# A new order and new engines for the first sixteen chunks of a gated recurrence with a feed-forward block

## The chip, the cores and the metric

The kernel runs on one core of one Trainium2 chip. The metric is the device time of one launch in microseconds (us). The core has five engines that work side by side, each through its own list of instructions, strictly in order: TensorE (PE, matrix products and transposes), VectorE (DVE), ScalarE (ACT, functions by table), GpSimd (POOL) and SyncE (SP, which here only issues DMAs). They wait for each other by semaphores alone.

## The reference

A linear recurrence over time runs through four sequences of 5824 tokens with 256 channels, and its output goes through a feed-forward block with a product in the middle and no nonlinearity:

```python
sig_r = 1.0 / (1.0 + np.exp(-r_gate)); sig_i = 1.0 / (1.0 + np.exp(-i_gate))
log_a = c * sig_r * np.log(np.clip(a_base, 1e-06, 1.0 - 1e-06))[None, None, :]
a_t = np.exp(log_a)
norm = np.sqrt(np.maximum(1.0 - a_t * a_t, 1e-06))
x_gated = norm * sig_i * x
for t in range(S):
    h = a_t[:, t] * h + x_gated[:, t]
    y[:, t] = h
a = y @ w1; b = y @ w2          # 256 -> 1024
return (a * b @ w3) @ w_out     # 1024 -> 1024 -> 256
```

All inputs and the output are float32. The kernel computes with bfloat16 operands on TensorE.

## The kernel before

The 23296 tokens are cut into 47 chunks, 0 to 46: chunks 0, 1 and 46 have 256 tokens, all others 512. Since nothing nonlinear stands between w3 and w_out, the kernel folds the two into one 1024x256 matrix `wp_sb` first (the eight "folds"), so each chunk needs only three products.

Nothing is left to a scheduler. A long string, `ORDER`, lists every job as a short word, and the kernel emits the jobs in exactly that order. Each engine so gets its own list: the words that belong to it, in the order of the string. Sets of tuples above the string (`DV_COPY`, `AC_SQUARE` and so on) say which engine does a job that several could do. The words, for chunk c, with the lines of the kernel before:

| word | job | engine (line) |
|---|---|---|
| r, i, x c | load of the r gate, the i gate, x, 512 KB each | SP (L136) |
| R, I c | tanh of the r gate (to bfloat16), of the i gate | ACT (L145/147, L154) |
| p c, t c.half | i gate plus 1; times x, to bfloat16 tile `u_t`; for chunks in `DV_TIMES` both in one | POOL (L159, L178) or DVE (L175, L178) |
| V, U c | turn tanh(r), turn u to channels x time | PE transposes to PSUM for chunks in `TURN_R` / `TURN_U` (L185), else a DMA transpose issued by SP (L196) |
| d c.half | decay a = exp(...) | ACT (L207) |
| s c.half | a squared | POOL or DVE (L217), ACT if in `AC_SQUARE` (L215) |
| q c | square root of 1 - a squared | ACT (L221), with its own function table |
| g c | times u | DVE (L229/232) |
| h c.half | the recurrence itself, a scan | DVE (L249) |
| y c | h to bfloat16 | POOL, DVE or ACT (L255/258) |
| a c.mp.q, b c.mp | quarter mp of y@w1 (one half each), of y@w2 | PE (L268) |
| c c.mp.q | copy of a from PSUM | DVE if in `DV_COPY` (L282), else ACT (L284) |
| m c.mp | product of the copy and b | DVE (L296) |
| D c.j, e c.j2, o c.j2 | product with `wp_sb`, copy from PSUM, store | PE (L307), ACT or DVE (L284/282), SP (L326) |
| L.., C.. | load and cast of weights | SP (L353); POOL, ACT or DVE (L360/362) |
| Ft, Fc, Fm, Fe mi | fold: 8 transposes, copy, 8 products, scale into `wp_sb` | PE (L367), DVE/ACT, PE (L378), DVE/ACT (L413/415) |
| W n | eight matmuls on nothing but the identity, whose result nobody reads | PE (L263) |

Tanh and exp share one of ACT's function tables and the root needs another, so ACT loads a table each time it goes from the one kind to the other. Copies and squares need no change of table.

Buffers are rings: `ring()` hands out the next slot of a tag each time a tile is taken, and a tile that comes back to a slot waits until the old content is done with. Four slots `po` of PSUM are shared by the turned gates, the folds, all `a` and all `D`; two slots `pb` by all `b` and `W`; three tiles `g` hold the products of three chunks, so m of chunk 3 cannot begin before D of chunk 0 is done. D needs all eight folds.

A chunk that is in both `TURN_R` and `TURN_U` is loaded with runs of 4 KB (`long_rows`), the others with runs of 1 KB.

## Time and profile before

| what | value |
|---|---|
| time, three runs | 515.61, 517.05, 517.40 us; median 517.05 us |
| profiled execution: its own time by the profile, the span from first to last instruction | 513.8 us |
| last matmul of TensorE | starts its last group at 507.24 us of the span |
| transposes for turned gates on PE (L185) | 104 |
| DMA transposes (L196) | 40 of r, 39 of u |
| DMA | 123.82 MB, mean 241 GB/s |

The three runs were not profiled, so the span is set beside their median: 3.2 us lie outside it. PE's matmuls overlap one another in the profile (each is shown with its whole time through the array), so what a matmul costs in a row of matmuls is the distance from one start to the next, not its duration. A few per cent of PE's matmul records are missing.

### The profile page before, as it was taken

To read this page: it belongs to the slowest core of one execution; us is meant where nothing else is said; L and a number is where in the kernel's file an instruction comes from. 1 tells how busy PE (TensorE), PEld (TensorE's weight loads), DVE (VectorE), ACT (ScalarE), POOL (GpSimd) and SP (SyncE) were. 2 spreads that over 40 slices of the span, in tenths; PEclk is the share of its full clock that TensorE was granted. 3 is DMA by queue.
4 is the path that set the end of the run, shared out by engine and by line. 5 is a ranking of instruction groups with operands and counts; after the bars stand their busy time and mean duration, and the time that the engine had idled before them with its cause. 6 is when DMAs were issued, how large, how long until landed. Compare 5 with 4: busy or idle time off the path is not lost.

```text
span 513.8 us, 9036 instructions
## 1 busy us (share of the span) xinstructions
PE 499.8 (97%) x3267; PEld 314.2 (61%) x3321; DVE 430.6 (84%) x414; ACT 465.5 (91%) x720; POOL 312.9 (61%) x271
## 2 busy tenths in 40 slices
...
GB/s 299 410 414 255 305 315 285 312 240 316 314 242 269 266 276 261 221 276 201 289 288 310 262 272 191 234 228 246 197 265 132 215 316 170 101 150 76 54 60 103
DMA packets 177281, 123.82 MB, mean 241 GB/s; under 512 B 86354, under 2 KB 172884, under 8 KB 177236
## 3 DMA queue, kind: packets, MB, share of 16 engines
...
## 4 chain that ended last, share of the span: by engine, by line
PE 86%; ACT 5%; DMA 4%; issue 2%; DVE 2%; SPq 1%; ACTq 0%; DVEq 0%
PE po L307 29%; PE pb L268 28%; PE pa L268 27%; DMA r_t<-in_r_gate_dram 4%; ACT sa L284 2%; PE pw L378 1%; PE ptr L185 1%; DVE g_t L296 1%; PE ptw L367 1%; ACT ot L284 1%; SPq L136 1%; DVE h_t L249 1%; ACT i_t L154 1%; ACT a_t L207 1%; ACT L154 0%
## 5 line engine op out<-in xcount | busy, mean ns | idle before, releaser
L296 DVE TENSOR_TENSOR g_t<-sa,pb 128x1024 bf16<-128x1024 bf16 (+1 forms) x188 | 219.0, 1181 | 62.0 <-PE pb L268 29.1
L268 PEld LDWEIGHTS <-w_sb 128*128 128x128 bf16 x1504 | 146.3, 98 | 146.8 <-issue 5.5
L284 ACT CAST sa<-pa 128x512 bf16<-128x512 f32 (+1 forms) x339 | 182.4, 588 | 27.6 <-PE pa L268 18.3
L268 PE MATMUL pa<-y_t,w_sb 128*128 128x512 bf16 (+1 forms) x721 | 185.9, 372 | 4.5 <-ACT sa L284 3.5
L268 PE MATMUL pb<-y_t,w_sb 128*128 128x512 bf16 (+1 forms) x729 | 182.5, 372 | 1.5
L307 PE MATMUL po<-wp_sb,g_t 128*128 128x256 bf16 x1456 | 177.7, 273 | 0.4
L307 PEld LDWEIGHTS <-g_t 128*128 128x128 bf16 x1456 | 142.4, 98 | 40.5 <-issue 0.9
L258 POOL CAST y_t<-h_t 128x1024 bf16<-128x1024 f32 (+1 forms) x46 | 51.2, 1112 | 141.2 <-DVE h_t L249 138.8
L178 POOL TENSOR_TENSOR u_t<-i_t,x_t 128x512 bf16<-128x512 f32 (+1 forms) x89 | 120.0, 1365 | 5.5 <-DMA ut<-u_t 2.5
L249 DVE TENSOR_TENSOR_SCAN h_t<-a_t,h_t,nrm 128x512 f32<-128x512 f32 (+1 forms) x92 | 121.0, 1345 | 1.9
L217 POOL TENSOR_TENSOR nrm<-a_t 128x512 f32<-128x512 f32 (+1 forms) x74 | 81.3, 1116 | 12.8 <-ACT a_t L207 9.9
L207 ACT ACTIVATE a_t<-rt,la 128x512 f32<-128x512 bf16 (+1 forms) x80 | 64.2, 821 | 0.0
L159 POOL TENSOR_SCALAR i_t<-i_t 128x1024 f32<-128x1024 f32 (+1 forms) x45 | 53.4, 1189 | 17.6 <-ACT i_t L154 17.6
L284 ACT COPY ot<-po 128x512 f32<-128x512 f32 (+1 forms) x85 | 49.6, 590 | 11.8 <-PE po L307 11.5
L232 DVE SCALAR_TENSOR_TENSOR nrm<-nrm,ut 128x1024 f32<-128x1024 f32 (+1 forms) x39 | 54.4, 1394 | 5.2 <-ACT nrm L221 5.2
L154 ACT ACTIVATE i_t<-i_t 128x1024 f32<-128x1024 f32 (+1 forms) x47 | 49.2, 1049 | 0.1
L221 ACT ACTIVATE nrm<-nrm 128x1024 f32<-128x1024 f32 (+1 forms) x47 | 48.4, 1040 | 0.2
L147 ACT ACTIVATE th_r<-r_t 128x1024 bf16<-128x1024 f32 (+1 forms) x40 | 42.6, 1065 | 0.0
L282 DVE CAST sa<-pa 128x512 bf16<-128x512 f32 (+1 forms) x37 | 21.9, 617 | 1.4 <-PE pa L268 1.1
L221 ACT ACT_TABLE_LOAD x17 | 21.8, 1283 | 0.4
L215 ACT ACTIVATE nrm<-a_t 128x512 f32<-128x512 f32 (+1 forms) x17 | 10.7, 648 | 0.1
L263 PE MATMUL warm<-ident 128*128 128x128 bf16 x128 | 10.2, 247 | 0.0
...
## 6 DMA issues: line engine op xcount, KB each, us to landing
...
```

Source lines behind the costliest of these rows:

```text
L154: nc.scalar.activation(out=t[:, :n, :], in_=t[:, :n, :], func=AF.Tanh, scale=0.5)
L159: (nc.vector if c in DV_PLUS else nc.gpsimd).tensor_scalar(t, t, 1.0, 1.0, op0=ALU.add, op1=ALU.mult)
L178: (nc.vector if (c, half) in DV_HALF else nc.gpsimd).tensor_mul(out=u, in0=t, in1=xt)
L207: nc.scalar.activation(out=a, in_=pr, func=AF.Exp, scale=la4[:, cb:cb + 1], bias=la4[:, cb:cb + 1])
L217: (nc.vector if (c, cb) in DV_SQUARE else nc.gpsimd).tensor_mul(out=n, in0=a, in1=a)
L221: nc.scalar.activation(out=T["n", c][:, :, :w], in_=T["n", c][:, :, :w], func=AF.Sqrt, scale=-1.0, bias=1.0)
L232: nc.vector.scalar_tensor_tensor(out=T["n", c][:, :, :w], in0=T["n", c][:, :, :w], scalar=1e-3, in1=T["pu", c][:, :, :w], op0=ALU.max, op1 ...
L249: nc.vector.tensor_tensor_scan(h[:, cb, :], a[:, cb, :], n[:, cb, :], init, ALU.mult, ALU.add)
L268: nc.tensor.matmul(out=dst[:, :w], lhsT=w_sb[:, cb, m * P:(m + 1) * P], rhs=T["y", c][:, cb, :w], start=(cb == 0), stop=(cb == NCB - 1))
L284: nc.scalar.copy(out=dst, in_=src_ps)
L296: nc.vector.tensor_mul(out=T["g", c][:, 2 * mp:2 * mp + 2, :w], in0=T["sa", c, mp][:, :, :w], in1=T["pb", c, mp][:, :, :w])
L307: nc.tensor.matmul(out=po, lhsT=T["g", c][:, k, j * P:(j + 1) * P], rhs=wp_sb[:, k, :], start=(k == 0), stop=(k == KD - 1), skip_group_che ...
```

## The change

It replaces the front of `ORDER`, up to its 701st word, by another arrangement of the same 701 words; the remaining 1763 words are the same. It moves jobs between engines by the sets. It takes chunks 7 and 12 out of `TURN_R` and chunk 5 out of `TURN_U`: V7, V12 and U5 become DMA transposes, and chunk 7 is loaded with runs of 1 KB. `W` stays at sixteen words of eight matmuls. Since halves of a job may now come in either order, a tile is taken by whichever half comes first ("if not in T") instead of by half 0; `pair` gives 2 for every chunk that uses it, and `FOLD_DMA` is empty, so neither changes an instruction.

The sets:

```diff
-    TURN_R = {0, 1, 2, 3, 4, 7, 12}
-    TURN_U = {0, 1, 2, 3, 4, 5, 6, 7}
+    TURN_R = {0, 1, 2, 3, 4}
+    TURN_U = {0, 1, 2, 3, 4, 6, 7}
     DV_TIMES = {0, 1}
-    DV_PLUS = set()
-    DV_HALF = {(2, 0)}
-    DV_SQUARE = {(0, 0), (1, 0), (10, 0)}
-    AC_SQUARE = {(1, 1), (2, 0), (2, 1), (3, 0), (4, 0), (4, 1), (6, 0), (8, 1), (9, 1), (11, 0), (11, 1), (12, 1),
-        (13, 0), (13, 1), (14, 0), (14, 1), (15, 1)}
-    DV_CAST = set()
-    AC_CAST = {4}
-    DV_COPY = {(0, 0, 0), (0, 1, 0), (0, 1, 1), (0, 3, 0), (1, 1, 0), (1, 1, 1), (1, 2, 0), (1, 2, 1), (1, 3, 0), (2,
-        0, 1), (2, 1, 0), (2, 1, 1), (2, 3, 0), (3, 0, 1), (3, 2, 0), (3, 2, 1), (4, 0, 0), (4, 1, 0), (4, 2, 0), (4, 2,
-        1), (5, 1, 1), (5, 2, 1), (6, 2, 0), (6, 2, 1), (6, 3, 1), (7, 0, 0), (7, 1, 1), (7, 3, 0), (7, 3, 1), (8, 1, 0),
-        (8, 2, 0), (9, 1, 0), (9, 1, 1), (9, 2, 1), (10, 0, 0), (10, 1, 0), (10, 1, 1)}
-    DV_EVAC = {(1, 0), (2, 0), (3, 1), (5, 1), (9, 0), (9, 1)}
-    FOLD_ACT = {('c', 7), ('e', 0), ('e', 1), ('e', 2), ('e', 3), ('e', 7)}
-    W_ACT = {('w2', 0), ('w3', 6)}
-    W_DVE = {('w1', 1)}
-    STAGE = {'w1': ['a', 'a'], 'w2': ['nrm', 'nrm'], 'wo': ['a', 'nrm'], 'w3': ['a', 'nrm', 'a', 'nrm', 'a', 'nrm',
-        'a', 'nrm']}
+    DV_PLUS = {2}
+    DV_HALF = set()
+    DV_SQUARE = {(1, 1)}
+    AC_SQUARE = {(2, 0), (2, 1), (3, 1), (4, 0), (4, 1), (5, 1), (6, 1), (7, 1), (8, 0), (8, 1), (10, 0), (10, 1),
+        (11, 0), (12, 0), (12, 1), (13, 0), (13, 1), (14, 0), (14, 1), (15, 1)}
+    DV_CAST = {0, 3}
+    AC_CAST = set()
+    DV_COPY = {(0, 0, 0), (0, 0, 1), (0, 1, 0), (0, 1, 1), (1, 0, 0), (1, 0, 1), (1, 1, 0), (1, 1, 1), (1, 2, 0), (1,
+        2, 1), (2, 0, 0), (2, 0, 1), (2, 1, 1), (2, 2, 1), (2, 3, 1), (3, 1, 0), (3, 1, 1), (3, 2, 0), (3, 2, 1), (3,
+        3, 0), (4, 0, 1), (4, 1, 0), (4, 1, 1), (4, 2, 1), (5, 0, 0), (5, 0, 1), (5, 1, 0), (5, 1, 1), (5, 2, 1), (6,
+        1, 0), (6, 2, 0), (6, 2, 1), (6, 3, 1), (7, 3, 0), (8, 0, 0), (8, 1, 1), (8, 2, 1), (8, 3, 1), (9, 0, 0), (9,
+        1, 0), (9, 1, 1), (9, 2, 1), (10, 0, 0), (10, 1, 0), (10, 1, 1)}
+    DV_EVAC = {(1, 0), (5, 1), (9, 0), (9, 1)}
+    FOLD_ACT = {('c', 3), ('c', 7), ('e', 2), ('e', 4), ('e', 5), ('e', 7)}
+    FOLD_DMA = set()
+    W_ACT = {('w2', 0), ('w2', 1), ('w3', 7)}
+    W_DVE = {('w1', 0), ('wo', 0)}
+    STAGE = {'w1': ['a', 'a'], 'w2': ['nrm', 'nrm'], 'w3': ['a', 'nrm', 'a', 'nrm', 'a', 'nrm', 'a', 'nrm'], 'wo':
+        ['a', 'nrm']}
```

The code, in one example of eight alike, and the two additions:

```diff
     def square(c, cb):
         w = sizes[c]
-        if cb == 0:
+        if ("n", c) not in T:
             T["n", c] = ring(held, [P, NCB, CT], F32, name="nrm", tag="nrm")
...
+    def pair(c, j2):
+        return min(2, sizes[c] // P - 2 * j2)
...
     def fold_t(mi):
+        if mi in FOLD_DMA:
+            T["w3t", mi] = ring(ffn, [P, KD, P], BF16, name="w3t", tag="w3t")
+            nc.sync.dma_start_transpose(out=T["w3t", mi], in_=T["w3b", mi][:, 0, :])
+            return
```

The start of the order:

```diff
-       r0 r1 E A3. A0. A1. i1 R1 R0 W3 V1 I1 V0 W13 W12 A2. W9 d1.0 d1.1 s1.0 i0 W15 I0 x0 t0.1 W14 d0.0 s0.0 s1.1
-       d0.1 s0.1 q0 x1 t1.1 Lw1.0 r3 Lw2.0 r2 q1 R3 Lw1.1 i2 W11 U0 g0 h0.0 Lw2.1 Cw1.0 W10 W2 U1 W0 W7 R2 W4 h0.1
-       Lw3.2 x2 g1 y0 W8 Lwo.0 Cw2.0 a0.1.0 a0.1.1 h1.0 c0.1.0 h1.1 a0.0.0 a0.0.1 V2 c0.1.1 d2.0 c0.0.0 W6 y1 b0.0
-       c0.0.1 d2.1 I2 Cw1.1 a1.0.1 a1.0.0 b0.1 a1.1.0 a0.2.0 c1.0.0 c1.0.1 Cw2.1 p2 a0.2.1 Cw3.2 m0.0 m0.1 c1.1.0
-       Lwo.1 b1.0 m1.0 t2.0 r4 W1 c0.2.0 a1.1.1 a0.3.0 t2.1 Cwo.0 W5 c1.1.1 Ft2 c0.2.1 a1.3.0 s2.0 b1.1 c0.3.0 b0.2
-       U2 a1.3.1 s2.1 Cwo.1 i3 Fc2 V3 x3 Lw3.0 q2 Lw3.1 i4 Lw3.4 m1.1 c1.3.0 Fm2 R4 g2 h2.0 h2.1 d3.0 Lw3.7 c1.3.1
-       m0.2 d3.1 Lw3.5 Fe2 a1.2.0 a0.3.1 b1.2 a1.2.1 I3 c0.3.1 V4 s3.0 d4.0 d4.1 b0.3 y2 c1.2.0 Cw3.0 c1.2.1 m1.2
-       a2.0.0 a2.1.0 b1.3 m0.3 a2.2.0 b2.0 m1.3 a2.2.1 c2.0.0 Lw3.3 a2.0.1 s4.0 c2.2.0 s3.1 p3 t3.0 c2.1.0 Cw3.1 Ft0
-       c2.0.1 c2.2.1 Fc0 m2.0 Cw3.4 b2.1 I4 s4.1 q4 r7 t3.1 a2.3.0 a2.1.1 Fm0 b2.2 p4 Cw3.5 c2.1.1 Ft4 c2.3.0 m2.1
-       Fe0 Ft1 a2.3.1 U3 Lw3.6 q3 Fc4 c2.3.1 Fc1 Fm4 Cw3.7 b2.3 Ft5 g3 Fe4 Fc5 Ft7 x4 Cw3.3 R7 r5 h3.0 h3.1 Fm1 Fm5
-       Fc7 Fe5 Ft3 Fm7 Fe1 Cw3.6 V7 Fe7 y3 Ft6 Fc3 d7.0 d7.1 Fc6 m2.2 Fm3 i6 r6 a3.1.0 Fe3 R5 Fm6 a3.1.1 c3.1.0
-       c3.1.1 t4.0 Fe6 t4.1 i7 i5 x5 U4 a3.0.0 R6 D0.0 a3.0.1 D0.1 I6 c3.0.0 e0.0 m2.3 g4 a3.3.0 a3.2.0 b3.0 h4.0
-       h4.1 b3.1 c3.0.1 m3.0 D1.0 a3.3.1 D1.1 I5 c3.3.0 y4 V5 r8 m3.1 a3.2.1 V6 b3.2 I7 e1.0 c3.2.0 c3.2.1 c3.3.1
-       b3.3 m3.2 m3.3 p5 a4.0.1 r9 a4.1.0 d5.0 d5.1 R8 d6.0 s6.0 s7.0 d6.1 p6 t5.0 p7 x6 x7 o0.0 a4.0.0 i10 V8 D2.0
...
+       r1 r0 i0 x0 i1 x1 Lw1.0 r2 A3. E A0. A1. A2. R1 R0 I0 t0.1 W2 W4 W9 V0 V1 W12 U0 W14 W3 W5 W13 W8 W10 d0.1
+       d1.0 d1.1 d0.0 I1 s1.1 t1.1 Cw1.0 s0.1 s0.0 s1.0 q0 q1 R2 i2 Lw2.0 I2 Cw2.0 U1 W11 W7 W15 g0 h0.1 h0.0 y0
+       a0.0.1 W6 g1 h1.1 h1.0 a0.0.0 a0.1.0 V2 W1 b0.0 y1 p2 c0.0.1 c0.0.0 a1.1.1 a1.1.0 c0.1.0 m0.0 b1.1 c1.1.1
+       c1.1.0 m1.1 d2.1 s2.1 d2.0 s2.0 q2 x2 Lw1.1 Lw3.2 t2.1 Cw1.1 t2.0 a1.0.1 a0.1.1 b0.1 a1.0.0 b1.0 c1.0.1 c0.1.1
+       m0.1 c1.0.0 m1.0 a0.2.0 a1.3.1 a0.2.1 a0.3.0 Lwo.0 Lw2.1 Lwo.1 r3 Cw3.2 Cwo.1 r4 c0.2.0 c0.2.1 c1.3.1 c0.3.0
+       Cwo.0 Cw2.1 U2 g2 W0 a1.3.0 Ft2 b1.3 a0.3.1 Fc2 Fm2 c1.3.0 R3 c0.3.1 m1.3 a1.2.0 V3 b0.2 b1.2 Fe2 R4 h2.0 h2.1
+       Lw3.0 Lw3.4 i3 x3 Lw3.1 Lw3.5 Lw3.7 Lw3.3 r7 Lw3.6 x4 i4 r5 m0.2 a1.2.1 V4 b0.3 c1.2.0 c1.2.1 m1.2 d3.0 d3.1
+       d4.0 d4.1 y2 s3.0 Cw3.0 Cw3.4 a2.0.0 a2.2.1 m0.3 c2.0.0 a2.0.1 b2.0 c2.2.1 a2.2.0 c2.0.1 m2.0 a2.1.0 Ft4
+       a2.3.0 Fc4 s4.0 I3 c2.2.0 c2.1.0 s4.1 a2.1.1 a2.3.1 c2.3.1 c2.1.1 c2.3.0 b2.2 Ft0 b2.1 s3.1 q3 q4 Fm4 p3 t3.1
+       t3.0 Cw3.1 m2.2 m2.1 Fc0 Ft1 Cw3.7 Fe4 Fc1 Cw3.5 U3 b2.3 Fm0 Ft5 Ft7 g3 Fe0 Fc5 Cw3.3 Fm1 h3.1 Fe1 h3.0 y3 Ft3
+       Cw3.6 Fm5 R7 Fc7 Fm7 Ft6 V7 r6 i6 Fc3 Fm3 Fe3 Fc6 m2.3 Fe7 Fe5 I4 a3.0.0 b3.0 a3.1.0 Fm6 c3.1.0 Fe6 R5 c3.0.0
+       d7.1 d7.0 a3.2.1 p4 t4.0 t4.1 c3.2.1 a3.2.0 a3.1.1 a3.0.1 U4 R6 c3.0.1 I6 i5 I5 V5 d5.0 r9 V6 c3.2.0 c3.1.1
+       s7.0 g4 h4.0 h4.1 D1.1 D0.1 D1.0 D0.0 b3.1 a3.3.1 a3.3.0 e1.0 d5.1 s7.1 e0.0 d6.0 R9 y4 r8 x5 p5 s6.0 s5.0
+       t5.1 t5.0 m3.0 a4.0.0 a4.1.0 b3.2 m3.1 c3.3.0 m3.2 s5.1 c4.0.0 c3.3.1 x7 x6 p6 t6.1 t6.0 r10 V9 b4.0 a4.0.1
+       a4.2.1 c4.1.0 c4.0.1 m4.0 b3.3 a4.1.1 m3.3 c4.1.1 a4.3.0 D2.1 b4.1 D2.0 c4.2.1 m4.1 b4.3 a4.3.1 a4.2.0 b4.2 R8
+       d6.1 s6.1 q7 q5 q6 e2.0 c4.3.0 c4.2.0 d9.1 U5 V8 o0.0 o1.0 i9 i8 i7 o2.0 d9.0 c4.3.1 D3.0 D2.2 D3.1 D2.3 U6 g5
...
```

## The prediction

> **What bounds the kernel now.** I read the page first: busy shares and the end of the work.
>
> ```profile
> span 513.8 us, 9036 instructions
> ...
> PE 499.8 (97%) x3267; PEld 314.2 (61%) x3321; DVE 430.6 (84%) x414; ACT 465.5 (91%) x720; POOL 312.9 (61%) x271
> ...
> PE 86%; ACT 5%; DMA 4%; issue 2%; DVE 2%; SPq 1%; ACTq 0%; DVEq 0%
> ```
>
> The third line is the chain that ended last: TensorE is 86% of it. But a busy PE is not a fast one, so I next took the timeline of PE over the first 30 us, and priced PE's list from it.
>
> ```profile
> 12.97 1.03 PE L268 MATMUL pa<-y_t,w_sb 128*128 128x256 bf16 x8
> ...
> 18.99 0.38 PE L268 MATMUL pa<-y_t,w_sb 128*128 128x256 bf16 x2 [1.10 <-ACT sa L284]
> ...
> 25.13 0.38 PE L268 MATMUL pa<-y_t,w_sb 128*128 128x256 bf16 x2
> 27.70 0.38 PE L268 MATMUL pa<-y_t,w_sb 128*128 128x256 bf16 x2 [2.19 <-ACT sa L284]
> 27.92 0.60 PE L268 MATMUL pb<-y_t,w_sb 128*128 128x256 bf16 x4
> 28.38 0.38 PE L268 MATMUL pa<-y_t,w_sb 128*128 128x256 bf16 x2
> 28.66 0.61 PE L185 MATMUL ptr<-ident,th_r 128*128 128x128 bf16 x8
> 29.10 0.60 PE L268 MATMUL pb<-y_t,w_sb 128*128 128x256 bf16 x4
> ```
>
> From start to start: eight transposes take 29.10 - 28.66 = 0.44 us (0.0557 each by the median of all), a matmul of 256 columns 0.109, one of 512 columns 0.2165. With these the whole list of PE (without W, which nobody reads) is 490.9 us. At 27.70 the list has done 8.9 us; the last matmul ends at 510.7. 510.7 - 27.7 = 483.0 us for the remaining 482.0: **after 27.7 us PE loses 1 us in all.** The 18.8 us lost lie before: 12.0 until the first useful product at 12.97, 6.8 between 12.97 and 27.70. At a2.0.0 (29.54, list at 10.6) the loss is 18.9, and at D0.0 (48.76, list at 29.9) still 18.9.
>
> Then the chain in order of time and ACT around the last wait:
>
> ```profile
> 13.91 10.40 DMA r_t<-in_r_gate_dram
> 24.37 1.28 ACT L145
> 25.67 1.06 ACT th_r L145
> ```
>
> The load of r4 lands at 24.3; R4 stands in ACT's list ahead of a copy that frees a PSUM slot, so PE waits 2.19 us. Last, the busy times by stage (us, then busy of PE, PEld, DVE, ACT, POOL, granted clock, DMA share, GB/s):
>
> ```profile
> 12.97:27.70 14.73, 10.30 (x113) 8.42 (x112) 12.36 (x21) 12.62 (x20) 7.50 (x8) 1.00 1.04 410
> 27.70:48.76 21.06, 20.90 (x196) 15.66 (x199) 18.19 (x27) 20.11 (x31) 15.76 (x15) 1.00 0.91 353
> 48.76:125.00 76.24, 75.78 (x491) 47.32 (x498) 74.43 (x79) 75.90 (x107) 50.26 (x45) 1.00 1.06 290
> ```
>
> From 48.76 to 125 PE, ACT and DVE are all full; PE can only come forward if ACT and DVE come forward too.
>
> **Part 1: three turns leave PE.** V7, V12 and U5 are 3 x 8 = 24 transposes: 24 x 0.0557 = **-1.34 us** on a list that has no gaps. *TensorE: Matmul & The Clock Gate*, Part 4, speaks of about 275 ns for such a transpose in a kernel; by that the sum here would be 24 x 0.275 = 6.6 us, an estimate from the page. The starts here stand 0.0557 apart, and the measurement decides. In their place SP issues three DMA transposes (1.28 us of issue each, landing 4.4 us later by the median). Of the gates of chunks 5 to 16 turned by DMA, the one with least room waits 2.2 us between landing and first reader and most wait 4 to 14, so I cost the three at nothing on the path; without that cover each costs up to the 4.4 us of its landing. The worst place is V7: in SP's list it waits for R7 with r6, i6, i5 and V5 behind it. By the walk below R7 ends near 40.8; r6 then lands near 44, R6 stands on ACT near 47, and before, the DMAs idle from 47.5 to 50 anyway. Decays from `rt` take 0.83 instead of 0.78 us: four of them, +0.2 us on ACT. Chunk 7's loads in 1 KB runs are not on the path: chunks 5 and 6 load so now.
>
> **Part 2: the first chunks.** I walk the new lists with the durations of before; landings by rank, since from 10.0 us on the DMAs land one 512 KB load each 1.25 us (w1.0 at 10.02, the tenth after it at 22.5).
> - Gates. R1, R0, I0, the four decays (0.45 each from 5.51), I1: ACT is at 7.9; table 1.28, q0 ends 9.85, q1 10.4 (before 10.78). w1.0 lands at 10.02 and is cast on DVE (0.6), g0 0.67, two scans 1.2, y0 on DVE (about 0.4, half of the 0.69 us cast of 1024): 12.95. The first product starts at **13.0, as before**.
> - ACT. Table, R2 (lands 11.3) 11.7 to 12.7, I2 to 13.6, cast of w2.0 (lands 13.8) to 14.8, two decays and two squares of chunk 2 (0.67, 0.56 each) to 17.3, table, q2 ends at **20.3; before 23.2**. R3 and R4 come later, when r3 (22.5) and r4 (23.8) are there: the two waits for loads (0.70 and 1.18) and the table load between are off the path.
> - DVE. g1, two scans to 14.8, p2 (0.6), six copies (0.31) and m0.0, m1.1 (0.6) to 18.2, m0.1, m1.0 to 20.3, cast of wo.0, g2 at 21.2 (before 23.8), two scans to 26.1 (27.4), y2 27.2 (28.5).
> - PE. b0.0 at 15.0, a1.1.1 waits for its slot until 15.8, U2 until 20.7 for the copy behind q2, b1.3 until 22.6 for the cast of w2.1, V3 until 25.3 for R3. a2.0.0 then starts at **27.8 with 11.1 us done: 16.7 lost, 2.2 less** than before. Going on alike (V4's slot, Fe4 and Fc7 on ACT cost PE 0.2 to 0.5 each), D1.1 starts at 48.7 with 31.6 done: 17.1 lost against 18.9. **-1.8 us.**
>
> All stretches here show a clock of 1.00 with PE gaps of up to 2.2 us; the walk's longest gap is the 1.8 us ahead of the first product, so the sum holds no loss of clock. *TensorE: Matmul & The Clock Gate*, Part 1, would speak against so thin a start: an idle window of about 3.4 us halves the clock until PE has been busy for about as long again; an estimate from the page is 3.4 us x 1/2 = 1.7 us more per fall. No run here shows one.
>
> **Part 3: do ACT and DVE follow?** Net of both lists in the changed part, by rows of before (start to start):
> - ACT: one weight cast and one fold copy more (0.95 each), four 512 squares (0.57) and two evacuations (0.53) more, against seven 512 copies (0.5), y4 (0.95), a 256 copy, a 256 square and an Fe (0.3 each), and the 0.2 above: nothing. Table loads stay as many. Its idle time until q12 falls from about 5.7 (1.3 is the start, 0.9, 0.7, 1.2 and 0.8 waits for loads and folds) to 2.5. ACT can be 3.2 us earlier.
> - DVE: seven 512 copies (0.6 each), a weight cast, y0, y3, a 256 copy and an Fe come, two evacuations, a fold copy, t2.0 (0.95) and two squares go; p2 is an operation that DVE did not do: its bounds are 0.69 (cast) and 1.26 (the 1024-wide g), and I take 0.6 start to start, as for the cast, the nearest. **+3.3 us.** Until m9.0 DVE idled 12.6 us; by the walk 6.2 stay. DVE can be 12.6 - 6.2 - 3.3 = 3.1 us earlier.
> - POOL gives up some 6 us and waits 18 us for h alone between 45 and 125: no bound.
>
> ```profile
> POOL y_t L258 <- DVE h_t L249: 18.1, 5, 4.3
> POOL i_t L159 <- ACT i_t L154: 11.7, 4, 5.1
> ```
>
> **Sum.** -1.34 - 1.8 = -3.1 us, just what ACT and DVE allow. Those two have no room left over 76 us, so I take 0.5 us of new stalls in chunks 5 to 15 (ends: -1.0, when the 1 us that PE loses now goes too, and +3, the 3.1 us of DVE room gone). **-2.6 us** on a span of 513.8: 511.2. The median of the runs is 3.2 us above the span; 517.05 - 2.6 = **514.4**.
>
> **Rivals.**
> - *The start is won and lost again.* ACT never waits between 45 and 125 and its work does not shrink. If chunks 5 to 15 hold jobs in a worse order, PE waits at PSUM slots until it stands where it stood; the 1.34 us of transposes then turn into waiting. For it: 75.9 of 76.2 us busy. Against: ACT's room of 3.2 us. Time 517.05 - 0 to 0.8: about 516.8.
> - *DVE becomes the bound: slower.* It takes 3.3 us more in the stage where it has 1.8 us of 76 free. If the 6.4 us of idle time that the walk saves in the first 45 us do not go, m9.0 starts 3.3 us later than its 116.8, and PE, two pb slots ahead at most, is held as long: 517.05 + 3.3 = 520.3. It decides from the point where DVE saves less than 3.3 us of idle time. Against: its longest early waits (1.43 us for the root of q0, 1.28 for b1.0) end sooner in the walk.
> - *The change does not do what it says*: excluded for the transposes, the new list has 24 fewer.
>
> **Numbers.** Forecast 0.66, won and lost 0.20, DVE-bound 0.14. A difference of 0.3%, 1.55 us, is about what these runs (spread 0.35%) can tell from none. The forecast case lies beyond it (513 to 515.5), the second within, the third beyond on the other side: faster 0.66, same 0.20, slower 0.14. The low end is ACT's 3.2 us and the 1 us of present stalls: 512.8. The high end reaches halfway into DVE's case, 518.6, which leaves some 0.05 below and 0.14 above.
>
> **What would show it.** Right: q2 ends near 20, a2.0.0 starts by 28.2, D1.1 by 49, L185 has 80 transposes, PE loses under 2 us after D1.1, the last matmul ends near 508. Wrong: PE gaps of over 1 us in 50 to 125 released by `sa`, `g_t` or `rt`; m9.0 later than 115; SP standing at V7 beyond 42 us while R6 or I5 wait for loads; a clock below 1.00 in the first 30 us.

## The result, and the profile after

The changed kernel takes **518.40 us** (median of 7 runs, 517.34 to 520.61); the kernel before, beside it on the same chip, 515.68 us (7 runs, 515.37 to 517.40). The ratio is **1.0046, with a 95% interval of 1.0026 to 1.0065**: slower by 0.46%, where 514.4 us and faster was forecast. In some executions of either kernel the clock stands at half for some 3.4 us of the start (the clock episode, see the last section); among those without it the median is 517.35 us for after (3 of the 7) and 515.5 to 515.8 us for before (in its four larger sets of executions), so the sign is the same and the difference some 1.7 us.

The page of after, lines as in the prediction:

```profile
span 516.5 us, 9044 instructions
...
PE 502.7 (97%) x3297; PEld 312.7 (61%) x3297; DVE 434.2 (84%) x420; ACT 466.6 (90%) x717; POOL 312.5 (61%) x267
...
PE 76%; ACT 7%; DMA 6%; DVE 5%; issue 2%; SPq 2%; POOL 1%; DVEq 0%; ACTq 0%; POOLq 0%
```

PE is again 97% busy, which says nothing. The chain that ended last says more: PE's share fell from 86% to 76%, and ACT, DMA and DVE took 7% of the span more. The span is 2.7 us longer although PE's list is 1.34 us shorter.

The timeline of PE over the first 31 us of after:

```profile
13.19 0.39 PE L271 MATMUL pa<-y_t,w_sb 128*128 128x256 bf16 x2 [1.14 <-DVE y_t L261]
...
20.70 0.38 PE L271 MATMUL pa<-y_t,w_sb 128*128 128x256 bf16 x2 [0.54 <-DVE sa L285]
...
25.54 0.62 PE L187 MATMUL ptr<-ident,th_r 128*128 128x128 bf16 x8 [0.38 <-ACT th_r L147]
...
27.98 1.46 PE L271 MATMUL pa<-y_t,w_sb 128*128 128x512 bf16 x6
```

The 2.19 us gap before R4 is gone, and chunk 2's first product starts at 27.98 instead of 29.54. The stretch tables of after, in the windows used for before (busy of PE, PEld, DVE, ACT, POOL, granted clock, DMA share, GB/s):

```profile
12.97:27.70 14.73, 12.34 (x134) 10.18 (x135) 14.35 (x27) 14.39 (x22) 7.28 (x7) 1.00 1.04 409
27.70:48.76 21.06, 21.06 (x182) 14.29 (x180) 20.17 (x31) 20.45 (x28) 14.85 (x15) 1.00 0.88 315
48.76:125.00 76.24, 73.82 (x474) 45.27 (x471) 72.93 (x77) 72.20 (x102) 43.05 (x40) 1.00 1.09 286
```

In the first row PE is busy 12.34 us instead of 10.30: the start was won. In the third, PE falls from 75.78 to 73.82, and ACT from 75.90 to 72.20: engines that were full now wait. For what, the waits from 45 to 130 us tell (us in total, times, longest):

```profile
POOL u_t L180 <- DMA x_t<-in_x_dram: 4.4, 2, 3.3
ACT a_t L209 <- DMA rt<-th_r: 2.3, 3, 0.9
DVE nrm L234 <- DMA ut<-u_t: 2.1, 2, 1.7
PE pb L271 <- DVE g_t L299: 1.9, 1, 1.9
PE pa L271 <- ACT sa L287: 1.8, 3, 1.1
ACT th_r L149 <- DMA r_t<-in_r_gate_dram: 0.9, 1, 0.9
```

In before, ACT and DVE wait for no DMA at all in this stretch, and POOL 0.3 us once. Here ACT waits 3.5 us (0.3 us of it for an i gate) and DVE 2.1 us for transfers, and PE then waits for copies and products that stand behind them. One by one, the waits are 0.38 us for V6, 0.32 for i8, 0.37 for U5, 0.95 for V12, 1.74 for U9, 0.93 for V15 and 0.90 for r17. Only U5 and V12 are turns that the change moved: 1.3 of 5.6 us. The other 4.3 us are waits for transfers that the kernel before makes as well, and does not wait for. Set against PE's list, PE now loses 6.7 us between the end of the start and chunk 46; before it lost 0.9 us there. (Summed again, the lists are 490.6 and 489.3 us; the prediction's 490.9 is 0.3 too high, which changes none of its differences.)

| us | before | predicted | after |
|---|---|---|---|
| q2 ends | 23.2 | 20.3 | 20.39 |
| a2.0.0 starts; PE has lost by then | 29.54; 19.0 | 27.8; 16.7 | 27.98; 17.0 |
| lost at the end of the start (D0.0 / D1.1, 48.7) | 19.0 | 17.1 | 17.2 |
| PE's list | 490.6 | -1.34 | 489.3 |
| lost between there and chunk 46 | 0.9 | about 1.5 | **6.7** |
| ACT's work until q12 | 129.7 | 0 more | 130.55 |
| DVE's work until m9.0 | 104.2 | 3.3 more | 107.16 |

### The profile page after: what moved, and what is told of

It reads as the page before. It is cut to its first block, busy times and chain, and to the rows that moved or that the text cites. A ratio compares the mean times of both kernels' runs of the same rounds, so it can differ in the third digit from the quotient of the medians.

```text
span 516.5 us, 9044 instructions
## 1 busy us (share of the span) xinstructions
PE 502.7 (97%) x3297; PEld 312.7 (61%) x3297; DVE 434.2 (84%) x420; ACT 466.6 (90%) x717; POOL 312.5 (61%) x267
## 4 chain that ended last, share of the span: by engine, by line
PE 76%; ACT 7%; DMA 6%; DVE 5%; issue 2%; SPq 2%; POOL 1%; DVEq 0%; ACTq 0%; POOLq 0%
PE pb L271 25%; PE pa L271 25%; PE po L313 24%; ACT sa L287 2%; DVE h_t L252 2%; DVE g_t L299 2%; DMA i_t<-in_i_gate_dram 2%; DMA r_t<-in_r_gate_dram 1%; DMA x_t<-in_x_dram 1%; PE pw L389 1%; ACT a_t L209 1%; SPq L198 1%; DMA out_dram<-ot 1%; SPq L138 1%; DVE sa L285 1%
## 5 line engine op out<-in xcount | busy, mean ns | idle before, releaser
L287 ACT CAST sa<-pa 128x512 bf16<-128x512 f32 (+1 forms) x331 | 178.2, 587 | 27.0 <-PE pa L271 18.5
L271 PE MATMUL pa<-y_t,w_sb 128*128 128x512 bf16 (+1 forms) x752 | 189.8, 372 | 4.8 <-ACT sa L287 2.0
L271 PE MATMUL pb<-y_t,w_sb 128*128 128x512 bf16 (+1 forms) x752 | 185.0, 372 | 2.6 <-DVE g_t L299 2.3
L180 POOL TENSOR_TENSOR u_t<-i_t,x_t 128x512 bf16<-128x512 f32 (+1 forms) x90 | 123.5, 1389 | 12.5 <-DMA ut<-u_t 4.6
L209 ACT ACTIVATE a_t<-rt,la 128x512 f32<-128x512 bf16 (+1 forms) x84 | 67.3, 817 | 2.7 <-DMA rt<-th_r 2.7
L234 DVE SCALAR_TENSOR_TENSOR nrm<-nrm,ut 128x1024 f32<-128x1024 f32 (+1 forms) x40 | 56.8, 1421 | 7.3 <-ACT nrm L223 4.8
L287 ACT COPY ot<-po 128x512 f32<-128x512 f32 (+1 forms) x87 | 50.7, 589 | 12.0 <-PE po L313 11.7
L156 ACT ACTIVATE i_t<-i_t 128x1024 f32<-128x1024 f32 (+1 forms) x47 | 48.7, 1042 | 1.3 <-DMA i_t<-in_i_gate_dram 1.2
L149 ACT ACTIVATE th_r<-r_t 128x1024 bf16<-128x1024 f32 (+1 forms) x42 | 44.5, 1059 | 1.0 <-DMA r_t<-in_r_gate_dram 0.9
L285 DVE CAST sa<-pa 128x512 bf16<-128x512 f32 (+1 forms) x45 | 26.4, 624 | 0.3
L217 ACT ACTIVATE nrm<-a_t 128x512 f32<-128x512 f32 x20 | 12.6, 636 | 0.2
```

Source lines behind the costliest of these rows:

```text
L180: (nc.vector if (c, half) in DV_HALF else nc.gpsimd).tensor_mul(out=u, in0=t, in1=xt)
L209: nc.scalar.activation(out=a, in_=pr, func=AF.Exp, scale=la4[:, cb:cb + 1], bias=la4[:, cb:cb + 1])
L234: nc.vector.scalar_tensor_tensor(out=T["n", c][:, :, :w], in0=T["n", c][:, :, :w], scalar=1e-3, in1=T["pu", c][:, :, :w], op0=ALU.max, op1 ...
L271: nc.tensor.matmul(out=dst[:, :w], lhsT=w_sb[:, cb, m * P:(m + 1) * P], rhs=T["y", c][:, cb, :w], start=(cb == 0), stop=(cb == NCB - 1))
L287: nc.scalar.copy(out=dst, in_=src_ps)
```

## The experiments

The question was where some 5.7 us between 50 and 150 us come from. The candidates, some with a letter in the expectations (C, D and G are explained there): **A**, the hole that SP's wait at V7 leaves in the transfers; **B**, the DMAs, full since before, which now get three turned tiles more, so that the new order's gates land too late; **E**, ACT's work is the bound; **F**, the order of DVE's and ACT's jobs by itself. "Lost later" is what PE loses between D1.1 and the first product of chunk 46, by the prices of the prediction, in the one profiled execution of each kernel.

| run | built on | ratio to before [95%] | lost later, us |
|---|---|---|---|
| before | | 1 | 0.9 |
| after | | 1.0046 [1.0026, 1.0065] | 6.7 |
| e1_loads_first | after | 1.0043 [1.0026, 1.0060] | 6.9 |
| e2_v7_on_pe | after | 1.0105 [1.0088, 1.0122] | 5.6, after 2.1 more in the start |
| e8_u5_pe | after | 1.0118 [1.0090, 1.0146] | 8.3 |
| e3_before_v7_dma | before | 1.0011 [0.9999, 1.0024] | 1.4 |
| e16_before_u5_dma | before | 1.0031 [1.0017, 1.0046] | 2.8 |
| e4_new_start_old_rest | both | 1.0071 [1.0057, 1.0086] | 5.6 |
| e5_g9_later | after | 1.0099 [1.0079, 1.0119] | 9.3 |
| e6_late_readers | after | 1.0089 [1.0063, 1.0114] | 8.5 |
| e9_no_act_squares | after | 1.0036 [1.0024, 1.0048] | 6.2 |
| e11_squares_pool | after | 1.0056 [1.0043, 1.0070] | 8.1 |
| e7_thin_stores | after | 1.0025 [1.0010, 1.0039] | 5.6 |
| e10_fewer_loads | after | 0.9974 [0.9962, 0.9987] | 4.3 |
| e14_fewer_loads_and_r | after | 0.9964 [0.9951, 0.9977] | 2.4 |
| e13_before_fewer_loads | before | 1.0008 [0.9993, 1.0022] | 0.5 |
| e15_fewer_loads_g9_later | after | 1.0091 [1.0071, 1.0111] | 8.6 |
| e12_before_copy_first | before | 0.9987 [0.9973, 1.0000] | 0.7 |

### The hole at V7

SP stands at V7 for 9.1 us, until 40.81, and the DMAs run dry behind it. The wait of SP's queue in after, and the stretch 41 to 44 us:

```profile
SPq L198 <- ACT w3t L287: 9.1, 1, 9.1
```

```profile
41.00:44.00 3.00, 3.00 (x33) 2.52 (x31) 2.39 (x4) 2.87 (x5) 0.00 (x0) 1.00 0.51 96
```

96 GB/s, where before moved 398. e1 puts the three loads ahead of V7:

```diff
-        Cw3.6 Fm5 R7 Fc7 Fm7 Ft6 V7 r6 i6 Fc3 Fm3 Fe3 Fc6 m2.3 Fe7 ... c3.0.1 I6 i5 I5 V5
+        Cw3.6 Fm5 R7 Fc7 Fm7 Ft6 r6 i6 i5 V7 Fc3 Fm3 Fe3 Fc6 m2.3 Fe7 ... c3.0.1 I6 I5 V5
```

> The changed kernel, with the words r6, i6, i5 moved ahead of V7: three loads are issued before SyncE stands waiting for R7. Nothing else moves. Theory A (the new wait of SP at V7, 9.1 us from 31.7 to 40.8, leaves the DMAs half empty from 38 to 44, and chunks 5 to 15 then get loads and turned gates just in time): the stretch 38 to 44 fills up, the loss of PE after D1.1 falls from 6.7 us to 3 or less, the span from 516.5 to about 513. Theory B (three more DMA transposes are too much for DMAs that are full from 45 to 130 anyway, wherever they stand): the loss stays above 5 us. Theory C (the new order of chunks 5 to 15 is worse for ACT and DVE by itself): unchanged, 516 to 517.

The same stretch of e1:

```profile
41.00:44.00 3.00, 3.00 (x33) 2.53 (x31) 2.42 (x4) 2.87 (x5) 0.00 (x0) 1.00 1.51 338
```

The hole is filled, yet at 60 us the DMAs have moved hardly more than in after (20.39 and 20.27 MB). The waits for V6 and U5 are gone, but the large stalls are the same: 1.9 us at b7.1 and 1.5 at a10.2.0. A falls as the cause by itself.

### One turn at a time

e2 and e8 give V7, or U5, back to PE in the new order; e3 and e16 take V7, or U5, to the DMAs in the old one. V12 alone was not tried.

```diff
-    TURN_R = {0, 1, 2, 3, 4}
+    TURN_R = {0, 1, 2, 3, 4, 7}
```

> The changed kernel with chunk 7 back in TURN_R: V7 is again 8 transposes on PE (0.45 us), SyncE does not wait for R7, chunk 7 loads runs of 4 KB again. Theory A: like the kernel with the three loads ahead of V7, span about 513. Theory B: one of three transposes and its DMA time gone, a third of the loss: span about 515. Theory C: 516.5 to 517.

```diff
-    TURN_U = {0, 1, 2, 3, 4, 6, 7}
+    TURN_U = {0, 1, 2, 3, 4, 5, 6, 7}
```

> The changed kernel with U5 back on PE (8 transposes, 0.45 us), a DMA transpose less. Theory B: a third of what the turns add goes, span 515 or less. Theory D: its wait at g5 (0.4 us) goes and the 0.45 us come back: no change, 516 to 517.

Both are slower still, by new stalls. PE's timeline of e2, then of e8:

```profile
48.21 1.03 PE L389 MATMUL pw<-wo_sb,w3t 128*128 128x256 bf16 x8 [0.95 <-ACT a_t L209]
```

```profile
68.11 1.14 PE L313 MATMUL po<-wp_sb,g_t 128*128 128x256 bf16 x9 [2.12 <-ACT sa L287]
```

A turn on PE holds one of the four `po` slots until ACT's decays (or DVE's g) have read it, and the new list has no slot free at these places: in e2 the fold Fm6 waits for the decays of chunk 7. So this pair says nothing on what the DMA turns cost. The old order does:

```diff
-    TURN_R = {0, 1, 2, 3, 4, 7, 12}
+    TURN_R = {0, 1, 2, 3, 4, 12}
```

> The kernel before with chunk 7 taken out of TURN_R and nothing else: V7 becomes a DMA transpose, and in the old list too it stands ahead of i6, r6, i7, i5, x5 and waits for R7 (ends at 41.6). Theory A: the same hole in the DMAs, here with five loads behind it, in an order that is not laid out for it: PE loses 2 to 6 us more, span 515.5 to 519.5. Theory B: one more transpose, up to 2 us slower. Theory C: 0.45 us faster, 513.4.

```diff
-    TURN_U = {0, 1, 2, 3, 4, 5, 6, 7}
+    TURN_U = {0, 1, 2, 3, 4, 6, 7}
```

> The kernel before with U5 alone turned by DMA (eight transposes fewer on TensorE, one DMA transpose more, chunk 5 not otherwise changed). The prediction's costing (a turn is worth -0.45 us and its DMA costs nothing): ratio 0.999, stalls after D1.1 as before, 0.9 us. Theory B: with the old order's room of 3 us and more at the gates it also costs little, 0.999 to 1.001. If a DMA turn costs by itself whatever the order (rival), chunk 5's g waits for it and the ratio is 1.002 or more.

V7 makes no difference that can be told from none. But at a cost of nothing it would have gained the 0.45 us by which PE's list is shorter, ratio 0.9991, and that lies outside its interval: its turn costs about what it saves, or more. U5 costs 0.31% although PE's list is 0.45 us shorter. DVE's timeline of e16, then PE's:

```profile
67.42 1.23 DVE L232 SCALAR_TENSOR_TENSOR nrm<-nrm,ut 128x1024 f32<-128x1024 f32 x1 [1.52 <-DMA ut<-u_t]
```

```profile
72.30 0.59 PE L268 MATMUL pa<-y_t,w_sb 128*128 128x512 bf16 x2 [1.35 <-POOL y_t L258]
```

U5 is issued 0.03 us after t5 and lands 3.5 us later. DVE is free for g5 1.5 us before that, and PE stands for y5 behind g5 and its scans. Here a DMA turn does stand on the path, by its own landing time.

### The new start before the old rest

e4 takes the first 274 words of the new order, then the old order with its engines, V7, V12 and U5 on PE. It changes too many words for a short diff; the sets of chunks 0 to 3 are the new ones, and:

```diff
-    TURN_R = {0, 1, 2, 3, 4}
-    TURN_U = {0, 1, 2, 3, 4, 6, 7}
+    TURN_R = {0, 1, 2, 3, 4, 7, 12}
+    TURN_U = {0, 1, 2, 3, 4, 5, 6, 7}
```

> The new order with its engines up to the word ahead of D1.1 (274 words), then the old order with its old engines for all words that are left; V7, V12 and U5 on PE as before. So the new start without a wait of SyncE for R7, and without the new order of chunks 5 to 15. Theory A and B: the 1.8 us won in the start stay, span about 512, up to 1 us lost at the seam. Theory C: the same. If the start is worth nothing because ACT and DVE cannot follow (the second case of the prediction): 513.8.

The lead lasts until 45 us; then PE waits 1.1 us at Fm6 and, by its timeline, here:

```profile
65.63 0.59 PE L266 MATMUL pa<-y_t,w_sb 128*128 128x512 bf16 x2 [2.43 <-ACT sa L282]
```

Here the earlier start is of no use to a rest that was arranged for the later one. By a6.0.0 PE has lost 22.8 us, against 18.9 in before. Neither ACT nor DVE waits for a transfer between 45 and 130 us in e4, so an order that does not fit loses 5.6 us without any late gate.

### Moving the job that waits, or those behind it

In after, DVE does g8, h8, g9 and h9 in a row ahead of m7.2, for which b7.1 waits. DVE's timeline of after, and PE's:

```profile
93.93 1.22 DVE L234 SCALAR_TENSOR_TENSOR nrm<-nrm,ut 128x1024 f32<-128x1024 f32 x1
95.25 2.46 DVE L252 TENSOR_TENSOR_SCAN h_t<-a_t,h_t,nrm 128x512 f32<-128x512 f32 x2
99.45 1.22 DVE L234 SCALAR_TENSOR_TENSOR nrm<-nrm,ut 128x1024 f32<-128x1024 f32 x1 [1.74 <-DMA ut<-u_t]
100.78 2.46 DVE L252 TENSOR_TENSOR_SCAN h_t<-a_t,h_t,nrm 128x512 f32<-128x512 f32 x2
103.15 2.33 DVE L299 TENSOR_TENSOR g_t<-sa,pb 128x1024 bf16<-128x1024 bf16 x2
```

```profile
104.40 1.02 PE L271 MATMUL pb<-y_t,w_sb 128*128 128x512 bf16 x4 [1.86 <-DVE g_t L299]
```

g9 waits 1.74 us for the turned tile of U9, and 5 us later PE waits 1.86 us. e5 moves g9 behind:

```diff
-        ... V14 g8 h8.0 h8.1 g9 h9.1 h9.0 y9 y8 t10.0 t10.1 t11.1 t11.0 p13 m7.2 b7.1 m7.3 e5.1 ...
+        ... V14 g8 h8.0 h8.1 y8 t10.0 t10.1 t11.1 t11.0 p13 m7.2 b7.1 m7.3 g9 h9.1 h9.0 y9 e5.1 ...
```

> The changed kernel with the words g9, h9.1, h9.0, y9 moved behind m7.3 and nothing else. Now DVE stands from 93.9 to 103.2 at g8, h8, g9, h9, waits 1.7 us in it for the turned u of chunk 9 (DMA), and PE waits 2.03 us at b7.1 for the products behind it. Theory D (what costs the time is the order on DVE and ACT: readers of DMA-turned gates placed ahead of work that PE waits for, while their data land just in time): the stall of 2 us at b7.1 goes, DVE's wait at g9 falls under 0.5, span about 514.5, unless the stalls at 126 to 128 (ACT waits for r17, V15) take over what was won: 515.5. Theory B (the DMAs are too full, whatever the order): the wait moves with g9, and under 0.7 us is won.

The wait only changes its place. PE's timeline of e5, then the stretch behind the stall:

```profile
110.86 0.59 PE L271 MATMUL pa<-y_t,w_sb 128*128 128x512 bf16 x2 [3.32 <-DVE ot L285]
```

```profile
110.86:114.30 3.44, 3.44 (x11) 1.34 (x11) 3.44 (x5) 2.93 (x3) 0.53 (x1) 0.66 1.01 325
```

e5.1, which frees a `po` slot, now stands behind g9 and h9. The granted clock (the number after the five engines) falls to 0.66 behind the stall: an episode at half clock of 3.41 us, which after does not have at this place, costs some 1.7 us of the 9.3 (half of 3.41, an estimate). So 9.3 is not the price of the stall alone; the same holds for e6 and e15 (clock 0.57 and 0.55 behind theirs). e6 also moves three readers of gates later on ACT:

```diff
-        ... V12 d12.1 R14 d13.0 D6.3 D6.2 a7.1.1 a7.1.0 e6.1 d13.1 c7.1.0 c7.1.1 b7.2 ...
+        ... V12 R14 d13.0 D6.3 D6.2 a7.1.1 a7.1.0 e6.1 d13.1 c7.1.0 c7.1.1 d12.1 b7.2 ...
-        ... d15.1 m8.3 a9.2.0 c9.1.0 b9.2 c9.1.1 R16 a9.2.1 ...
+        ... m8.3 a9.2.0 c9.1.0 b9.2 c9.1.1 R16 d15.1 a9.2.1 ...
-        ... D8.0 R17 t12.1 ... e8.0 c10.0.1 g11 ...
+        ... D8.0 t12.1 ... e8.0 c10.0.1 R17 g11 ...
```

> As the one with g9 later, and on ACT three readers of late data moved back as well: d12.1 behind c7.1.1, d15.1 behind R16, R17 behind c10.0.1. Theory D: the three waits of ACT at DMAs (0.9 us each at 100, 118 and 125 us) shrink and the two stalls of PE at 126 and 128 (1.8 us) go too: span about 512.5, below the kernel before by about 1 us. Theory B: waits come back at other readers; span above 515.

It does not help: 3.6 us at the same a8.1.1. So the expectation that the order of these readers could be mended by itself failed both times.

### ACT's work

e9 leaves out the fifteen squares on ACT in chunks 5 to 15 (8.4 us of work; the root then takes 1 - a, so the outputs are others):

```diff
+        if (c, cb) in AC_SQUARE and 5 <= c <= 15:
+            return
```

> The changed kernel without the 15 squares that ACT does in chunks 5 to 15 (the root is taken of 1 - a there; left out of the computation): 15 x 0.56 = 8.4 us less work on ACT between 50 and 145, nothing moved. Theory E (ACT is the bound of this stage: up to q12 it works 0.85 us more than before, and each wait for a DMA, 3.5 us after 48.7, is paid in full because it has no idle time to give; PE follows it, +3.0 us): PE's loss after D1.1 falls from 6.7 to 2 or 3 us, span about 512.5. Theory F (DVE is the bound, with its 3 us of new work): loss stays above 5 us, span over 515.

If ACT's work were the bound, all 5.7 us should go. The time moves by 0.1% of before's, no more than the intervals leave open. The waits of e9 from 45 to 130 us:

```profile
ACT a_t L209 <- DMA rt<-th_r: 3.2, 3, 1.2
ACT i_t L156 <- DMA i_t<-in_i_gate_dram: 2.1, 2, 1.2
DVE nrm L237 <- DMA ut<-u_t: 2.0, 2, 1.3
ACT th_r L149 <- DMA r_t<-in_r_gate_dram: 2.0, 1, 2.0
```

ACT's waits for DMAs rise from 3.5 us to 7.3: with less to do it arrives sooner at gates that have not landed. E falls, and the waits point to B. e11 gives squares of chunks 7, 8, 10 and 12 (five in all) to POOL instead, with nothing left out:

```diff
-    AC_SQUARE = {(2, 0), (2, 1), (3, 1), (4, 0), (4, 1), (5, 1), (6, 1), (7, 1), (8, 0), (8, 1), (10, 0), (10, 1),
-        (11, 0), (12, 0), (12, 1), (13, 0), (13, 1), (14, 0), (14, 1), (15, 1)}
+    AC_SQUARE = {(2, 0), (2, 1), (3, 1), (4, 0), (4, 1), (5, 1), (6, 1), (8, 1),
+        (11, 0), (12, 1), (13, 0), (13, 1), (14, 0), (14, 1), (15, 1)}
```

> The changed kernel with six squares of chunks 7 to 12 on POOL instead of ACT, nothing else: 3.4 us less on ACT, 6 us more on POOL, which waits for the scans most of the time there. Theory E: up to 3 us faster than the changed kernel, 513.5 to 515, if the multiplications on POOL behind those squares do not come late; F: no change or slower.

ACT does 2.1 us less and idles 6.8 us between 48.7 and q12 instead of 4.1, and PE loses more.

### Less for the DMAs to do

e7 stores 16 of 256 columns, so most of the output is not written:

```diff
-        nc.sync.dma_start(out=out[t0:t0 + k * P, :].rearrange("(j p) c -> p j c", p=P),
-                          in_=T["ot", c, j2][:, :k])
+        nc.sync.dma_start(out=out[t0:t0 + k * P, :16].rearrange("(j p) c -> p j c", p=P),
+                          in_=T["ot", c, j2][:, :k, :16])
```

> The changed kernel, but the stores of all chunks but the last write only 16 of the 256 columns (the output is left incomplete): the same instructions and waits, with some 17 stores between 45 and 130 us that take a sixteenth of the bytes, at least 5 us less DMA time there, as much as the change adds. Theory B: the DMA-turned gates and loads land sooner, the waits of ACT and DVE for DMAs (6.5 us between 45 and 130) go, the span falls to 512 or 513. Theory D: transfers are late because of the place of their issue in SP's list, not for want of DMA time: waits at V12, U9, V15 stay above half of what they were, span over 515.

The span is 515.4 us, so by the expectation this speaks for D and not for B. The waits are mixed: V12 falls from 0.95 to 0.11 us and r17 from 0.90 to 0.07, U9 from 1.74 to 0.95, V15 stays at 1.00. The gain is not clear of noise either: the intervals of e7 and after overlap, and among executions without the clock episode the medians are 517.5 and 517.35 us.

e10 also loads no x for chunks 8 to 19 (they take the x of chunks 4 to 7):

```diff
+        if nm == "x" and 8 <= c <= 19:
+            T["x", c] = T["x", 4 + c % 4]
+            return
```

> The changed kernel with the thin stores and without the loads of x for chunks 8 to 19 (they reuse x of chunks 4 to 7): besides the stores some 12 x 1.6 = 19 us less DMA time between 55 and 150, so that the DMAs are no longer full. Theory B: all waits of ACT and DVE for DMAs after 60 us go, PE's loss after D1.1 falls to 2 us, span 512. Theory G (the turned gates come late because R and t come late, in a chain that does not depend on how full the DMAs are): V12, U9, V15 are waited for as in the changed kernel, span over 514.

The waits for V15 and r17 go, but those for V6, U5 and U9 do not (0.61, 0.82 and 0.97 us), and PE still loses 4.3 us: a clear gain, but not the 512 us of B.

e13 does to the kernel before what e10 does to after:

> The kernel before with the same relief of the DMAs as in the run of after with fewer loads: stores write 16 of the 256 columns and chunks 8 to 19 load no x (they take the x of chunks 4 to 7), so most of the output is not computed. Theory B (the DMAs are full, and the new order's tight gates pay for it): the kernel before loses only 0.9 us after D1.1, so the relief gives it little, at most 0.5 us: ratio 0.998 to 1.001, and after with the relief, 0.9974, is no better for its order than this. Rival (the relief speeds any order alike): the kernel before gains the same 2.5 to 3 us as after did, ratio near 0.994 to 0.995.

e14 is e10 without the r loads of chunks 8 to 19 as well:

```diff
-        if nm == "x" and 8 <= c <= 19:
-            T["x", c] = T["x", 4 + c % 4]
+        if nm in ("x", "r") and 8 <= c <= 19:
+            T[nm, c] = T[nm, 4 + c % 4]
```

> After with thin stores and neither x nor r loads for chunks 8 to 19 (they take those of chunks 4 to 7), so the output is not complete. It takes another 15 us of DMA time from chunks 8 to 19. If late gates are behind what still stalled with fewer loads (104: 1.27 us, 143: 0.67), those stalls go and the ratio falls to 0.994 or below, with the 57 and 79 stalls (chunks 4 to 6, not relieved) left. If the order of DVE and ACT is behind them (theory F), they stay at 1 to 1.3 and 0.5 to 0.7 us and the ratio stays within 0.001 of 0.9974.

The stretch 48.76 to 125 us of e10, e14 and e13, with the DMA share as the last number but one (1.09 in after, 1.06 in before):

```profile
48.76:125.00 76.24, 73.52 (x468) 45.49 (x474) 73.25 (x77) 74.40 (x105) 46.09 (x42) 1.00 0.89 214
48.76:125.00 76.24, 74.97 (x481) 46.64 (x489) 75.00 (x79) 75.33 (x107) 46.54 (x42) 1.00 0.64 149
48.76:125.00 76.24, 75.78 (x492) 46.98 (x499) 74.28 (x79) 75.90 (x108) 50.41 (x46) 1.00 0.84 202
```

In the profiled executions e7, e10 and e14 give after back 1.1, 2.4 and 4.3 us of the 6.7 lost later; the first step is not clear of noise. In e14 neither ACT nor DVE waits for a transfer between 45 and 130 us. The control for e10, e13, gains nothing (1.0008 [0.9993, 1.0022]), so this is not a gain that any kernel would have. e14 has no control of its own, but the kernel before loses only 0.9 us there in all, so no relief could give it more than that. That e10 and e14 stand below 1 is in part the clock: 0 of 10 and 1 of 11 of their executions have the episode, 14 of 29 and 18 of 29 of before beside them. Without it they are 0.6 and 1.2 us faster than before.

DVE's timeline of e14 over the stretch shown above, then PE's:

```profile
93.94 1.22 DVE L237 SCALAR_TENSOR_TENSOR nrm<-nrm,ut 128x1024 f32<-128x1024 f32 x1
95.26 2.46 DVE L255 TENSOR_TENSOR_SCAN h_t<-a_t,h_t,nrm 128x512 f32<-128x512 f32 x2
97.64 1.20 DVE L237 SCALAR_TENSOR_TENSOR nrm<-nrm,ut 128x1024 f32<-128x1024 f32 x1
98.94 2.46 DVE L255 TENSOR_TENSOR_SCAN h_t<-a_t,h_t,nrm 128x512 f32<-128x512 f32 x2
101.31 2.33 DVE L302 TENSOR_TENSOR g_t<-sa,pb 128x1024 bf16<-128x1024 bf16 x2
```

```profile
102.56 1.02 PE L274 MATMUL pb<-y_t,w_sb 128*128 128x512 bf16 x4
```

The same five jobs in the same order: without the 1.74 us ahead of g9 the products end 1.84 us earlier, and b7.1 follows without a gap of note. So F, DVE's row of four jobs by itself, does not make this stall; I had expected that it might.

A rival is that fewer loads also make SP's list shorter, so that the turns are issued earlier. SP's timeline of U9, after and then e14:

```profile
92.92 1.24 SPq L198 DMA_TRANSPOSE ut<-u_t  x1
```

```profile
92.93 1.24 SPq L201 DMA_TRANSPOSE ut<-u_t  x1
```

U9 is issued at the same time and lands at 99.36 in after, at 97.19 in e14: for this stall it is the transfer. For V6, too, the issue ends at the same time and the landing comes 1.7 us earlier. At V12 and V15 the issue ends 1.3 and 1.6 us earlier in e14, so there SP's list has its part. The landing times in the same stretch (45 to 130 us, median us from issue to landing) show what the relief did. After, then e14:

```profile
rt<-th_r SPq DMA_TRANSPOSE x11, 5.5
ut<-u_t SPq DMA_TRANSPOSE x6, 4.7
```

```profile
rt<-th_r SPq DMA_TRANSPOSE x12, 2.9
ut<-u_t SPq DMA_TRANSPOSE x7, 3.7
```

e15 puts e5's move on top of e10:

> After with thin stores and no x loads for chunks 8 to 19 (output not complete), and g9, h9, y9 moved behind m7.3. With full DMAs this move cost 2.8 us more. If DVE's row g8 to h9 ahead of m7.2 is by itself worth the 1.27 us stall at b7.1 once gates land early (theory F), that stall goes and the ratio is 0.995 to 0.996. If the move breaks another wait also with relieved DMAs (e5.1 behind it on DVE, a8.1.1), a stall of 2 to 3.5 us at a8.1.1 stays and the ratio is above 1.000.

The stall at a8.1.1 stays, 4.1 us, with the half clock behind it: that move is wrong with full DMAs and with relieved ones.

### A small move in the kernel before

e12 puts the copy that PE awaits for 2.19 us ahead of R4:

```diff
-        ... m1.1 c1.3.0 Fm2 R4 g2 h2.0 h2.1 d3.0 Lw3.7 c1.3.1
+        ... m1.1 c1.3.0 Fm2 c1.3.1 R4 g2 h2.0 h2.1 d3.0 Lw3.7
```

> The kernel before with one word moved: c1.3.1, the copy that PE waits 2.2 us for, stands ahead of R4 on ACT instead of behind it and its wait for the load of r4. PE's gap ahead of a0.3.1 falls below 0.5 us; PE then has 1.8 us of work until y2 (28.5) and waits there, so a2.0.0 comes at 28.6 instead of 29.5. If the start decides: 0.9 us faster, and fewer executions in which the clock of TensorE falls for 3.4 us after that gap (1.3 us each). If ACT is the bound of the next stage, the 0.9 us are lost there again, since ACT's own order of work only shifts: no change.

0.9987 [0.9973, 1.0000] can hardly be told from no change. In its profile PE waits 2.1 us at a1.2.1 instead: the slot of V4, behind R4. It has the lowest ratio of the kernels here that compute everything; none is clearly faster than before. What differs is the clock: 2 of its 12 executions have the episode, 14 of the 29 of before beside it; without it the medians are 515.6 and 515.8 us.

## Why the prediction was wrong

**The base of the sum:** some 1.4 us too high, and not part of the change. Each execution on record whose span is listed took 1.7 to 2.4 us longer than its span, mostly 1.8 to 1.9; so the span of 513.8 belongs to a time near 515.7, which is the median of before beside after (515.68). The "3.2 us" set an execution without the clock episode beside a median that has, by its value, the episode in it (517.05; 517.07 is the median with it). The forecast change was -2.6 us; the measured one is +2.7.

**Part 1, the work that leaves PE:** right. 80 transposes at L187, PE's list 489.3 us.

**The step that failed: the room between a landing and its reader, "2.2 us and most 4 to 14".** It was read from the old order, and the new order was credited with it. Two terms rest on it: "I cost the three at nothing on the path" in Part 1, and the "0.5 us of new stalls in chunks 5 to 15" of the sum. In after the reader starts 0.13 us after the landing of V5, 0.02 for V6, 0.12 for U5, 0.09 for U9, 0.27 for U10, 0.03 for V15 and 0.02 for r17. The largest wait, at U9, shows both orders. DVE's timeline of before, where the reader of U9 (g9) waits for nothing:

```profile
104.12 1.22 DVE L232 SCALAR_TENSOR_TENSOR nrm<-nrm,ut 128x1024 f32<-128x1024 f32 x1
```

U9 lands at 95.92 there, 8.2 us ahead of g9. In after it is issued 3.1 us later and lands at 99.36, while DVE is ready for it at 97.7. The time from issue to landing is nearly the same, 6.1 and 6.4 us: it is the order that has lost the room.

**Part 1, the cost of nothing:** wrong even in the old order. V7's turn costs about the 0.45 us that it saves (e3); U5's, whose reader is ready 1.5 us before it lands, costs 0.31% on top of what it saves (e16). The prediction also priced only the landing time, not what a turn takes of the DMAs, whose share in 48.76 to 125 was already 1.06. By the packets, one turned tile (256 KB in 1024 packets of 25 ns, the mean of the whole run) takes 1.6 us of all sixteen engines, as much as a load of 512 KB in 1 KB runs. Three make 4.8 us; chunk 7's loads take 0.3 us more each in 1 KB runs. From 45 to 130 us the packets take 92.8 us of sixteen engines where they took 86.9. Not all of that is the three turns: this stretch holds 17 turned tiles after and 16 before, and loads have moved into it. The Trainium skill (*VectorE: DVE Perf Modes*, The three transpose paths) puts the DMA transpose at about 90% of DMA bandwidth. By bytes, the turned tile here runs at half the rate of the load, and the measurement decides.

**Part 1, the worst place:** V7 leaves SP at 40.81, as worked out (40.8), but the cost was not there (e1).

**Part 2, the start:** right, 1.8 us as predicted, term by term in the table above.

**Part 3, the work of ACT and DVE:** nearly right (0.85 us more on ACT where nothing was forecast, 2.97 on DVE for 3.3).

**Part 3, "0.5 us of new stalls in chunks 5 to 15":** the term that was mis-sized. PE's losses there grew by 5.7 us. The larger ones in after: 0.5 at a4.0.1 (57 us), 0.4 at D4.2, 0.5 around 79, 2.0 at b7.1 (104), 1.8 at a10.0.1 and a10.2.0 (126 and 128), 0.9 at a12.0.0 (146). ACT idled 1.6 us less up to 48.7, but 3.7 us more after it; DVE 4.1 less, then 1.5 more. The end of the range, +3, was drawn from DVE's work and left out that ACT and DVE can wait for transfers. The stalls at 126 and 128 show the way from a late gate to PE. ACT's timeline of after, then PE's:

```profile
117.75 0.81 ACT L209 ACTIVATE a_t<-rt,la 128x512 f32<-128x512 bf16 x1 [0.93 <-DMA rt<-th_r]
...
124.80 1.06 ACT L149 ACTIVATE th_r<-r_t 128x1024 bf16<-128x1024 f32 x1 [0.90 <-DMA r_t<-in_r_gate_dram]
```

```profile
126.38 0.59 PE L271 MATMUL pa<-y_t,w_sb 128*128 128x512 bf16 x2 [0.39 <-ACT sa L287]
128.09 0.59 PE L271 MATMUL pa<-y_t,w_sb 128*128 128x512 bf16 x2 [1.11 <-ACT sa L287]
```

Two waits of 0.9 us, at V15 and r17, stand in ACT's list ahead of the copies that free the slots for chunk 10. Both waits are gone in e10 and e14; the 1.27 us at a10.2.0 goes with them in e10 and falls to 0.37 in e14.

**Sum:** -1.34 - 1.8 + 5.7 = +2.6 us; the spans differ by 2.7.

**The rivals:** "won and lost again" has the shape of what happened, but it was stopped at the old time, by ACT's order, with no DMA in it; and DVE, which idles 1.5 us more in that stage than before, was not the bound. Of the signs named, PE gaps over 1 us released by `sa` and `g_t`, and m9.0 at 117.2, came as the signs of a wrong forecast; SP did not stand at V7 beyond 42 us.

**How far the cause is shown:** with the controlled relief (e10 against e13) the new order loses 4.3 - 0.5 = 3.8 us more than the old one, where without relief it loses 5.7 more: one third of the loss goes. With the stronger relief (e14) 2.4 us are left, of which the old order's own share can be 0 to 0.9, so 1.5 to 2.4 us: about two thirds of the loss come from transfers that land late in an order that reads them as they land. These are figures of one profiled execution each; by the medians without the clock episode, with the 3.1 us of the list and the start taken as won, they are about a half for e10 and 60% for e14. The rest, as far as it lies between 45 and 130 us (1.3 us of it before 104), is no late gate of ACT or DVE, since in e14 these two wait for no transfer there; it is left for the order of the jobs, and e4 shows that an order alone can lose that much. Open is how the loss divides between the three turns and the new arrangement, since no version of the new order with all turns on PE was run; the waits in after stand for the greater part (4.3 of 5.6 us) at transfers that the change did not add, but the added ones may have made those late.
